# Half of a load moved forward on GpSimd's queue, and small corrections moved from VectorE to ScalarE, in a Fourier-mixing and channel-mix kernel

## The chip, the cores and the metric

The kernel runs on one core of a Trainium2 chip. The metric is the device time of one execution in microseconds (us). Every time was taken on one core, and every run was of the state called fast (no run was over 1.5% above the fastest of its kernel).

## The reference

Each of 8 batches (3072 rows of 256 columns) is Fourier-transformed along both axes, of which the real part is kept; a channel mix with the row before follows.

```python
X = np.fft.fft(x, axis=1)
x = np.fft.fft(X, axis=2).real
x_prev = np.concatenate([zeros, x[:, :-1, :]], axis=1)
xk = mu_k * x + (1.0 - mu_k) * x_prev
xr = mu_r * x + (1.0 - mu_r) * x_prev
k = np.maximum(xk @ w_k, 0.0)           # 256 -> 1024
v = k * k @ w_v                         # 1024 -> 256
r = 1.0 / (1.0 + np.exp(-(xr @ w_r)))   # 256 -> 256
return (r * v).astype(np.float32)
```

## The kernel before

The transform is done in stages on TensorE: A (sums over one index, by `a_sum` or, after a butterfly on VectorE, by `a_item`), D (`w_eo`, the transform along the columns) and C (tables `m1`, `m2`). VectorE forms the mixes, then K (`wk`), R (`wr`) and V (`wv`) are the products of the channel mix. All tables are computed on the chip during the first 43 us or so: angles on VectorE, sines on ScalarE, the last slices and the tables of the 128-row product (`tw`, `u128`) on GpSimd. GpSimd also issues every load of x and the weights, in the order of its program. K's weights come in two sets, and the rows of wk and wr are gathered in the order in which the transform leaves its columns.

```python
def loads():                                   # GpSimd's queue, at the start
    for a in range(2):
        next(row_part)                         # row numbers, 4 small operations
        gather(wk_sb[0][a], moe_w_k, a)
    nc.gpsimd.dma_start(out=wv_sb, in_=...)
    load_xh(1, 0)                              # batch 1's x, first half
    for a in range(2):
        gather(wr_sb[0][a], moe_w_r, a)
    load_xh(1, 1)
    next(row_part)
...
at(4, m_last)          # GpSimd: the last tables, four operations
at(4, loads_2)         # GpSimd: two gathers of wk, two of wr
at(5, plain_128)       # GpSimd: tw, u128
at(6, butterfly, 1, 1, 0)                      # VectorE
at(8, load_xh, 2, 0)   # GpSimd: batch 2's x
at(10, load_xh, 2, 1)
```

`eo_rest` writes two columns of `w_eo`; `m_ends` turns the sign of 64x64 pieces of `m1` and `m2` and zeroes a column of each. Both are on VectorE and are shown in the diff.

## Time and profile before

| | the kernel before |
|---|---|
| median of the first three timed runs (range) | 457.66 us (457.11 to 458.13) |
| the profiled execution | 455.39 us, span 453.6 us, clock 1.0 |
| TensorE busy | 444.9 us, 98% of the span |

The prediction below shows the lines of the shares, of the chain of waits up to stage D and of GpSimd's timeline at the start. GpSimd's timeline of the kernel before around 40 us (start, us, engine, line, operation, tiles, number, and in brackets the idle time before it with what ended it): the last gather of wr, three of the first four operations on `tw`, and batch 2's x.

```profile
35.48 0.95 POOL L364 DMA_INDIRECT wr<-in_moe_w_r_dram,row_i  x1 [0.30 <-issue]
...
38.60 1.25 POOL L407 TENSOR_SCALAR tw<-m 64x26 f16<-64x26 f16 x3 [0.20 <-issue]
...
43.48 1.15 POOL L104 DMA_DIRECT2D xh<-in_x_dram  x2
```

GpSimd has no idle time over 0.3 us here, and TensorE is busy without a gap from 44 to 80 us.

### The profile page before, as it was taken

What the parts mean: (1) busy time and instruction counts of PE and PEld (TensorE: products, weight loads), DVE (VectorE), ACT (ScalarE), POOL (GpSimd) and SP (SyncE); (2) the same over time, 40 slices, a digit from 0 to 9 for tenths busy, and PEclk for the clock granted to TensorE, in tenths of its full rate; (3) what the DMA queues carried; (4) which work ended last, traced back from release to release, by engine and by line L of the source; (5) the groups of instructions that cost most, each with busy time, mean ns of one, the idle gap of its engine ahead of it and who ended that gap; (6) DMA issues with size and microseconds to landing.
All of it is one profiled execution on the core that took longest, in us unless ns stands there. A gap on an engine that the chain in (4) does not pass through costs nothing.

```text
span 453.6 us, 9753 instructions
## 1 busy us (share of the span) xinstructions
PE 444.9 (98%) x4082; PEld 326.8 (72%) x4082; DVE 357.0 (79%) x499; ACT 360.7 (80%) x409; POOL 37.7 (8%) x71
## 2 busy tenths in 40 slices
PE   8899999999999999999999999999999999999995
PEld 5677777777777777777777777777777777676764
DVE  8999879977797869877788867887779755997453
ACT  7898997888778887888887888788878888666661
POOL 8748000000000000000000000000000000000000
PEclk9999999999999999999999999999999999999999
DMA  8975853537322572226522266122222222222223
GB/s 139 135 134 95 187 129 59 129 58 154 100 64 60 93 163 60 62 57 136 120 67 52 71 123 134 48 72 48 71 48 71 52 65 52 68 69 71 71 69 94
DMA packets 32412, 40.25 MB, mean 89 GB/s; under 512 B 3822, under 2 KB 29936, under 8 KB 31024
## 3 DMA queue, kind: packets, MB, share of 16 engines
q1 hardware_dynamic: 27776, 25.07, 22.0%
q0 software_dynamic: 4432, 14.42, 18.8%
q8 instruction: 32, 0.52, 0.5%
q10 hardware_dynamic: 160, 0.13, 0.1%
q14 instruction: 12, 0.10, 0.1%
HBM read 28.84 MB, written 25.17 MB: 119 GB/s over the span
## 4 chain that ended last, share of the span: by engine, by line
PE 94%; ACT 2%; DMA 1%; DVE 1%; issue 0%; POOL 0%; POOLq 0%
PE psV L623 37%; PE psW L585 36%; PE psW L609 9%; PE psW L458 4%; PE psW L434 4%; PE psW L489 3%; DMA xh<-in_x_dram 1%; ACT g_all L422 1%; ACT rl L595 1%; DVE a L420 1%; PE psW L448 1%; ACT L614 0%; ACT pq L422 0%; ACT r L614 0%; DVE rl L318 0%
## 5 line engine op out<-in xcount | busy, mean ns | idle before, releaser
L595 ACT ACTIVATE rl<-psW 128x1024 f16<-128x1024 f32 x192 | 196.4, 1026 | 79.6 <-PE psW L585 79.3
L623 PE MATMUL psV<-wv_sb,k 128*128 128x256 f16 x1536 | 198.6, 272 | 0.0
L585 PE MATMUL psW<-x,wk 128*128 128x512 f16 (+1 forms) x776 | 196.6, 377 | 0.3 <-ACT rl L595 0.3
L602 DVE TENSOR_TENSOR k<-rl 128x2048 f16<-128x2048 f16 (+1 forms) x98 | 117.5, 1202 | 61.3 <-ACT rl L595 60.6
L623 PEld LDWEIGHTS <-k 128*128 128x128 f16 x1536 | 143.7, 98 | 20.0
L585 PEld LDWEIGHTS <-wk 128*128 128x128 f16 x776 | 75.9, 98 | 50.2 <-issue 0.6
L633 DVE SCALAR_TENSOR_TENSOR o<-psV,r 128x512 f32<-128x512 f32 (+1 forms) x97 | 66.2, 683 | 23.8 <-PE psV L623 21.8
L554 DVE TENSOR_TENSOR x<-y,t 128x1536 f16<-128x1536 f16 x60 | 57.5, 958 | 2.1
L422 ACT ACTIVATE a<-psW 128x768 f16<-128x768 f32 x61 | 49.0, 806 | 1.6 <-PE psW L448 1.3
L609 PE MATMUL psW<-wr,x 128*128 128x256 f16 x384 | 49.8, 273 | 0.0
L614 ACT ACTIVATE r<-psW 128x1024 f16<-128x1024 f32 x48 | 49.0, 1020 | 0.8 <-PE psW L609 0.8
L609 PEld LDWEIGHTS <-x 128*128 128x128 f16 x384 | 37.6, 98 | 14.4
L422 ACT ACTIVATE g_all<-psW 128x1024 f16<-128x1024 f32 (+1 forms) x47 | 47.9, 1027 | 0.0
L117 DVE TENSOR_TENSOR eo<-xh 96x2048 f16<-96x2048 f16 x26 | 31.5, 1214 | 1.4 <-DMA xh<-in_x_dram 1.4
L458 PEld LDWEIGHTS <-a 128*128 128x128 f16 x384 | 25.0, 98 | 10.5 <-ACT a L422 0.6
L434 PEld LDWEIGHTS <-eo 96*128 96x128 f16 x416 | 23.4, 97 | 11.6
L104 POOL DMA_DIRECT2D xh<-in_x_dram x20 | 10.7, 539 | 222.6 <-DVE eo L117 221.7
L422 ACT ACTIVATE pq<-psW 128x896 f16<-128x896 f32 (+5 forms) x34 | 28.8, 851 | 0.5 <-PE psW L489 0.4
L458 PE MATMUL psW<-w_eo,a 128*128 128x128 f16 x376 | 28.3, 219 | 0.3 <-ACT rl L595 0.3
L434 PE MATMUL psW<-w_pm,eo 96*128 96x96 f16 x416 | 26.3, 205 | 0.0
L489 PEld LDWEIGHTS <-g_all 128*128 128x128 f16 x459 | 17.8, 98 | 8.4 <-ACT g_all L422 1.7
L489 PE MATMUL psW<-m,g_all 128*128 128x64 f16 x442 | 19.3, 193 | 0.9 <-ACT g_all L422 0.7
(107 smaller groups left out, 169.5 us busy)
## 6 DMA issues: line engine op xcount, KB each, us to landing
out_dram<-o SPq DMA_DIRECT2D x190, 128.0 KB, 2.4
xh<-in_x_dram POOLq DMA_DIRECT2D x14, 768.0 KB, 6.8
xh<-in_x_dram POOLq DMA_DIRECT2D x2, 384.0 KB, 5.3
xh<-in_x_dram POOLq DMA_DIRECT2D x4, 192.0 KB, 5.0
wv_sb<-in_moe_w_v_dram POOLq DMA_DIRECT2D x1, 512.0 KB, 8.6
out_dram<-o ACTq DMA_DIRECT2D x2, 64.0 KB, 2.0
out_dram<-o SPq DMA_DIRECT2D x2, 64.0 KB
y<-f SPq DMA_DIRECT2D x7, 3.4 KB
```

The lines of the kernel that those rows point to most:

```text
L422: nc.scalar.activation(out=out_ap, in_=in_ap, func=AF.Copy)
L434: nc.tensor.matmul(out=ps[:, 128 * i:128 * i + 96], lhsT=eo[:, 8 * j + i, e, :], rhs=w_pm[0:96, 0], start=True, stop=True)
L458: nc.tensor.matmul(out=_v(ps, 256 * i + 64 * (1 - e), [(128, 2), (1, 64)]), lhsT=a_t[b][:, e, 2 * u:2 * u + 2, :], rhs=w_eo[:, e, :], star ...
L489: nc.tensor.matmul(out=ps[:, o + 64 * i:o + 64 * i + 64], lhsT=g_all[:, u, col:col + 128], rhs=m[:, sl] if sl != 1 else mz[:, 0 if m is m1 ...
L554: V.tensor_tensor(out=dst, in0=_v(y_t[b], 64 * (NSL * a + lo + 3 * m), [(1, n)]), in1=_v(x_t["t", a], 64 * lo, [(1, n)]), op=ALU.subtract ...
L585: nc.tensor.matmul(out=st["k", ds][:, 512 * hs + lo:512 * hs + hi], lhsT=wk_sb[m][a][:, 128 * fc:128 * fc + 128], rhs=xk[:, a, 512 * i + l ...
L595: nc.scalar.activation(out=st["rl"][:, 2 * ds:2 * ds + 2], in_=st["k", ds].rearrange("p (f t) -> p f t", f=2), func=AF.Relu, bias=0.0, sca ...
L602: V.tensor_tensor(out=k2_t[c][:, lo:hi], in0=r, in1=r, op=ALU.mult)
L609: nc.tensor.matmul(out=ps[:, 256 * tb:256 * tb + 256], lhsT=x_t[b, 1, m][:, a, 512 * i + 128 * tb: 512 * i + 128 * tb + 128], rhs=wr_sb[m] ...
L614: nc.scalar.activation(out=st["r", c], in_=ps, func=AF.Sigmoid)
L623: nc.tensor.matmul(out=st["v", tb - h][:, 256 * h:256 * h + 256], lhsT=k2_t[c][:, fc, 128 * tb:128 * tb + 128], rhs=wv_sb[:, fc], start=(f ...
L633: V.scalar_tensor_tensor(out=o.rearrange("p a b -> p (a b)")[:, 0:256 * n], in0=st["v", t0][:, 0:256 * n], scalar=16.0, in1=st["r", c][:, ...
```

## The change

Its intent: VectorE ends stage A of batch 0 late, so the two corrections of w (`eo_rest`) and of the tables (`m_ends`) go to ScalarE, into its waits, and the last part of the second angles goes behind stage A. The first half of batch 1's first x is put at the head of the queue, right behind batch 0's x.

```diff
--- before.py
+++ after.py
@@ -333,14 +333,15 @@
         V.tensor_scalar(out=m2[lo64, s0:s1], in0=m1[hi64, s0:s1], scalar1=-1.0, scalar2=None,
                         op0=ALU.mult)
         V.tensor_copy(out=m2[hi64, s0:s1], in_=m1[lo64, s0:s1])
+        if s0 == 0:
+            for m in (m1, m2):
+                V.memset(m[:, 0, 0:1], 0.0)
 
     def m_ends():
 
 
-        for n, m in enumerate((m1, m2)):
-            V.tensor_scalar(out=m[hi64, 0], in0=m[hi64, 0], scalar1=-1.0, scalar2=None,
-                            op0=ALU.mult)
-            V.memset(m[:, 0, 0:1], 0.0)
+        for m in (m1, m2):
+            nc.scalar.activation(out=m[hi64, 0], in_=m[hi64, 0], func=AF.Copy, scale=-1.0)
 
     def m_zero():
         for n, m in enumerate((m1, m2)):
@@ -366,12 +367,15 @@
 
     V.memset(mz, 0.0)
 
+    xh_t[1, 0] = xh_pool.tile([96, 16, 256], FP16, name="xh")
+
     def loads():
+        load_part(1, 0, 0, 8)
         for a in range(2):
             next(row_part)
             gather(wk_sb[0][a], moe_w_k, a)
         nc.gpsimd.dma_start(out=wv_sb, in_=moe_w_v.rearrange("(fc p) v -> p fc v", p=128))
-        load_xh(1, 0)
+        load_part(1, 0, 8, 8)
         for a in range(2):
             gather(wr_sb[0][a], moe_w_r, a)
         load_xh(1, 1)
@@ -391,8 +395,8 @@
     def eo_rest():
 
         for col, sign in ((63, 0.5), (127, -0.5)):
-            V.tensor_scalar(out=w_eo[:, 0, col:col + 1], in0=w_eo[:, 0, 127:128], scalar1=sign,
-                            scalar2=0.5, op0=ALU.mult, op1=ALU.add)
+            nc.scalar.activation(out=w_eo[:, 0, col:col + 1], in_=w_eo[:, 0, 127:128],
+                                 func=AF.Copy, bias=0.5, scale=sign)
 
     def plain_128():
 
@@ -644,6 +648,7 @@
 
     loads()
     eo_sine()
+    eo_rest()
     a_sum(0, 0, 0)
     a_sum(0, 0, 4)
     keep_busy(1)
@@ -655,11 +660,10 @@
     a_sum(0, 1, 0, "V")
     a_sum(0, 1, 4)
     m_zero()
-    eo_rest()
-    m_angles(22, NSL)
     a_sum(0, 1, 8)
     a_sum(0, 1, 12, "V", 2)
     a_sum(0, 1, 14, "A", 2)
+    m_angles(22, NSL)
     m_ends()
     mu_turn()
     d_half(0, 0, ps_v(), "A")
```

## The prediction

> **What bounds the kernel now.** The kernel takes 457.66 us (457.11 to 458.13); the profiled execution has a span of 453.6 us, all at the full granted clock. I read the page's shares first.
>
> ```profile
> PE 444.9 (98%) x4082; PEld 326.8 (72%) x4082; DVE 357.0 (79%) x499; ACT 360.7 (80%) x409; POOL 37.7 (8%) x71
> PE 94%; ACT 2%; DMA 1%; DVE 1%; issue 0%; POOL 0%; POOLq 0%
> ```
>
> The second line is the chain that ended last. TensorE is busy for 98% of the span and is 94% of that chain. The rest of the chain (ACT, DVE, DMA) lies almost all before 40 us, and every line of the diff works there, before 20 us or so. So the change cannot touch the steady part: it can only shift its start. All of TensorE's idle time is 453.6 - 444.9 = 8.7 us; by stretches, 1.55 us of it is before 6 us, 0.52 in 6 to 12 us and 1.33 in 12 to 20 us. A gain can come above all out of these last two.
>
> Next I read the chain of waits in order of time up to 40 us (columns: start, us, what).
>
> ```profile
> 8.18 0.85 PE psW L448 x8
> 9.05 0.96 DVE a L420
> 10.01 0.40 DVE rl L318
> 10.44 0.44 DVE m L333
> 10.91 0.73 DVE m L335
> 11.68 0.96 DVE a L420
> 12.64 0.07 DVE w_eo L394
> 12.73 0.16 DVE w_eo L394
> 12.89 0.40 DVE rl L318
> 13.29 0.48 DVE a L420
> 13.90 0.61 PE psV L458 x8
> ```
>
> From 9.05 to 13.77 us VectorE is the bound: its last piece of stage A (L420, ended 13.77) waits behind the two corrections of w (L394) and a part of the second angles (L318), and stage D (L458) starts at 13.90 only because of it. This is what the change goes for. Last I read the timeline of GpSimd, which issues all loads, with the first use of wk on TensorE beside it (columns: start, us, engine, line, what).
>
> ```profile
> 6.64 1.39 POOL L192 TENSOR_SCALAR unit<-pcol_i 2x1 f32<-2x1 int32 x2
> 8.12 0.71 POOL L290 TENSOR_SCALAR row<-pcol_f 128x1 f32<-128x1 f32 x1
> 10.11 1.28 POOL L364 DMA_INDIRECT wk<-in_moe_w_k_dram,row_i  x1 [0.29 <-POOL row_i L293]
> 12.95 1.29 POOL L364 DMA_INDIRECT wk<-in_moe_w_k_dram,row_i  x1 [0.27 <-POOL row_i L298]
> 14.23 0.99 POOL L373 DMA_DIRECT2D wv_sb<-in_moe_w_v_dram  x1
> 15.20 0.61 POOL L104 DMA_DIRECT2D xh<-in_x_dram  x1
> 19.19 3.62 PEld L585 LDWEIGHTS <-wk 128*128 128x128 f16 x26
> ```
>
> To see here: GpSimd is a strict queue that runs without a pause from 1.26 to 20.9 us; behind the row numbers (L290 to L298) it issues wk's two gathers, wv, then batch 1's x. TensorE takes up wk at 19.19 us without waiting for it.
>
> [...] So a load with an unmet wait holds up everything behind it on GpSimd. The trace before has no such case among these loads (no idle of GpSimd there over 0.3 us); it has the mild form, the wk gather waiting 0.29 us for its row numbers. [...] L290 took 0.71 us beside VectorE's wrap of the angles (8.01 to 8.74), the like operations after it 0.27, 0.24 and 0.21. [...] The trace before shows gaps of at most 0.63 us after the start and no fall; the gap that I predict is near 1.2 us, so I count nothing for it.
>
> **The change part by part.**
> (1) w's corrections to ScalarE, right behind its sine (5.22 to 5.73). ScalarE then waits 1.28 us for TensorE until 7.01; two operations of one column at 0.20 us each (its 128x1 activation at 2.04 took that) fit in. Cost 0; VectorE's chain loses 12.64 to 12.89, 0.25 us.
> (2) The last angles (0.40 us in the chain) go behind VectorE's last piece of A: that piece ends 0.65 us sooner in all, less some 0.08 for the two memsets (0.06 each, overlapping) that now come before the A evictions: about 13.77 - 0.57 = 13.2.
> (3) m's sign corrections go to ScalarE behind its last A eviction, which ends at 13.30. Two 64x64 operations at 0.20 us (mz's two took 0.39) end at 13.70, before stage D's first result could be there. Hidden.
> Stage D then waits for ScalarE's eviction at 13.30 and for TensorE's small mu products, whose modelled end is 13.35: it starts at about 13.42 in place of 13.90. **Gain: about 0.5 us**, which the chain D, C, K would carry on to K's first product, 18.7 in place of 19.2.
> (4) The load of batch 1's first half is put ahead of the row numbers on GpSimd. The buffer is that of batch 0's first x (two buffers, two halves in use), and the built program has the load wait for TensorE's count 43, ten warm-up products plus all 33 up to the end of L448's fourth group, the buffer's last reader. In the trace that count arrives at 9.69 us. GpSimd is free at 8.05. So it stands still for 1.65 us, issues for 0.55 (its loads of x take 0.53 to 0.66) and starts L290 at 10.3 in place of 8.12: **2.2 us later**, and L290 then meets VectorE's angles, swap and copy (9.93 to 11.64), so 2.0 to 2.7 after the blocking is counted. All gathers shift with it. The first wk gather goes from 10.11 to about 12.35, the second from 12.95 to about 15.25.
>
> When does wk land? In the trace's landing records the first gather's last increment is at 14.81, 4.70 us after its start; of the second's, at least 17.59, 4.64 after (11 of its 16 are missing). The second would land at 15.25 + 4.64 = 19.9 (19.5 to 20.4). K's second product needs it; before, that ran at about 19.3 with 1.7 us of slack. The shift of 2.2 to 2.3 us eats this slack and 0.6 us more. So K starts at about 19.9, TensorE standing idle from 18.8, and **the 0.5 us of (1) to (3) ends in this wait**.
> After that, ScalarE is busy for 8.00 of the 8.00 us from 20 to 28 and TensorE for 7.82 of the next 8.00, so a late K isn't caught up. wv (landed 22.88, used at 25.00) moves by 2.3 but has less x beside it and is used 0.6 later: about even. The gain of the early half of x is nil: L448 took it up at 27.68 without a wait, as all of it had landed at 26.70.
> Sum: -0.5 (hidden) and +0.6 at K: 457.66 + 0.6 = **458.3 us**.
>
> **The rivals.**
> Rival A, the intent: wk lands in time and the 0.5 us stays. For it: part of the second gather's 4.64 us may be queueing, the DMA engines stand nearly idle at 11 and at 14 us, and few landings are recorded; the row operations may slip through between VectorE's. It needs the shift plus the flight to be 1.2 us shorter than I have it. It makes 457.66 - 0.5 = 457.2.
> Rival B, the wait is longer: GpSimd's row operations are blocked up to 11.64 by VectorE's swap, and the x load of 384 KB (some 2 us at the 200 GB/s that x's loads show) is ahead of wk's packets. Then wk lands at 20.5 and wv too comes late (25.5 against 25.2). For it: the 1.2 us that GpSimd's second operation of L192 took against 0.22 of the first; against it: the engines should be through with that half by 13.1 us, before wk's first packet. It makes +1.2 to +1.5, 459.0.
> Rival C, no engine or wait matters: the gain and the wait cancel and the result is 457.7.
>
> **Range and chances.** The three medians lie within 1.1 us of each other: 457.2 (a quarter), 457.7 to 458.5 (half), 459 (a quarter), each with run-to-run noise of some 0.5 us, as the times before spread. So 458.3 with a range from 456.9 to 459.3. 2% is 9.2 us, more than all of TensorE's idle time, so a gain of that size is out of the question; a loss of it would need a wait ten times my estimate or a fallen clock. Chances: faster 0.01, within 2% 0.98, slower 0.01.
>
> **What would show it.** Right: L394's successors stand on ScalarE before 7 us; stage D starts near 13.4; GpSimd's new load starts near 9.7 behind a wait for TensorE of about 1.6 us; the second wk gather starts near 15.2; the first L585 weights (a shifted line number) show a wait for a DMA of about 1 us and start near 19.9; a total within 1 us of before. Wrong: no idle time of TensorE ahead of K (then rival A, and the step that failed is the landing of wk); GpSimd not held at the new load (then the wait on count 43 was misread); stage D still at 13.9 (then the gain of (1) to (3) was not there to lose); or a wait at wv's first use (rival B).

Where a cut is marked, the text held a statement on the hardware that no trace or run shows. The sum came to -0.5 (hidden) and +0.6 at K, 457.66 + 0.6 = 458.3 us. Three of its arguments need their numbers beside them. That a load with an unmet wait holds up what stands behind it on GpSimd was taken for granted; the changed kernel's trace shows it: GpSimd stands 1.99 us for TensorE ahead of the new load, and L290 behind it starts at 10.64 us in place of 8.12. What is called blocking there is read from the durations alone: L290's 0.71 us, and L402, an operation of one column too, took 1.26 us beside VectorE's square (36.60 to 37.81 us) in the kernel before and 0.25 us in the profile of only_moves (L403 there, at 38.62 us), where it came after the square; in the changed kernel L290 and L291 took 0.38 and 0.39 us beside the swap and the copy. And that a gap near 1.2 us costs no clock was my assumption; the trace has no such gap after the start. In the rivals, the DMA engines that "stand nearly idle" have a share of 0.31 from 11 to 12 us and of 0.27 from 14 to 15, and x's loads moved 184 to 205 GB/s from 4 to 10 us.

## The result

The changed kernel takes **455.44 us** (455.23 to 456.17, six executions), against 457.38 us (456.85 to 458.13, six) of the kernel before in the same rounds. The ratio is 0.996 with a 95% interval of 0.9947 to 0.9974. Here and below, a ratio is the mean time of one kernel's runs over that of the other's of the same rounds, so not quite the ratio of the medians that I quote. The class, within 2%, is as predicted; the time is 1.5 us below the low end of the range.

The profiled execution of the changed kernel took 456.13 us (span 454.4), that is 0.74 us **more** than the profiled one of the kernel before. Its shares and the engines of its chain:

```profile
PE 444.6 (98%) x4082; PEld 326.6 (72%) x4082; DVE 356.1 (78%) x495; ACT 361.7 (80%) x413; POOL 38.1 (8%) x72
PE 92%; DMA 2%; ACT 2%; POOL 1%; issue 1%; DVE 0%; POOLq 0%
```

TensorE is as busy as before, and DMA and POOL have come into the chain. Where, the chain of waits of the changed kernel shows (start, us, what):

```profile
10.02 0.56 POOL xh L104
...
12.43 1.10 POOL wk L365
...
15.05 4.97 DMA wk<-in_moe_w_k_dram,row_i
20.07 1.39 PE psW L589 x11
```

The early half of x is followed by the gathers of wk, and the second gather's landing (15.05 + 4.97 = 20.02) releases K. The timelines of the same kernel, of GpSimd, ScalarE and TensorE in this order:

```profile
10.02 0.56 POOL L104 DMA_DIRECT2D xh<-in_x_dram  x1 [1.99 <-PE psW L452]
15.05 1.07 POOL L365 DMA_INDIRECT wk<-in_moe_w_k_dram,row_i  x1 [0.27 <-POOL row_i L298]
```
```profile
5.76 0.44 ACT L398 ACTIVATE w_eo<-w_eo 128x1 f16<-128x1 f16 x2
13.39 0.40 ACT L344 ACTIVATE m<-m 64x64 f16<-64x64 f16 x2
```
```profile
13.42 0.62 PE L462 MATMUL psV<-w_eo,a 128*128 128x128 f16 x8
20.07 4.42 PE L589 MATMUL psW<-x,wk 128*128 128x256 f16 x27 [0.54 <-DMA wk<-in_moe_w_k_dram,row_i]
```

Stage D starts at 13.42 us in place of 13.90, but GpSimd stood 1.99 us for TensorE ahead of the new load, and K now waits 0.54 us for wk. Every step in the trace is the one predicted, and yet the timed runs are 2 us faster. So the gain is in executions that these two traces don't show, and the experiments had to find those.

### The profile page after: what moved, and what is told of

The parts are those of the page before. It is cut to its first block, busy times and chain, and to the rows that moved or that the text cites. A ratio compares the mean times of both kernels' runs of the same rounds, so it can differ in the third digit from the quotient of the medians.

```text
span 454.4 us, 9755 instructions
## 1 busy us (share of the span) xinstructions
PE 444.6 (98%) x4082; PEld 326.6 (72%) x4082; DVE 356.1 (78%) x495; ACT 361.7 (80%) x413; POOL 38.1 (8%) x72
## 4 chain that ended last, share of the span: by engine, by line
PE 92%; DMA 2%; ACT 2%; POOL 1%; issue 1%; DVE 0%; POOLq 0%
PE psV L627 37%; PE psW L589 35%; PE psW L613 9%; PE psW L462 4%; PE psW L438 4%; PE psW L493 3%; ACT rl L599 1%; DMA xh<-in_x_dram 1%; DMA wk<-in_moe_w_k_dram,row_i 1%; PE psW L452 1%; ACT g_all L426 0%; ACT L618 0%; POOL xh L104 0%; POOL wk L365 0%; ACT r L618 0%
```

## The experiments

Seventeen runs were made, five of them repeats of a kernel; the runs of one call share a chip and the runs of the kernel before, and each call had another chip. Where its row in a table says "before", those are the shared runs. Each timed run of five rounds gives six executions (a_third seven), the first of which is the profiled one.

### First call: both kernels again, and the two halves of the change

`b_again` and `a_again` are the kernels before and after, unchanged. 

> The kernel before once more, unchanged, for the spread of its own executions and a second trace: the first profiled execution took 455.39 us, 2.0 us less than the median of the timed ones (457.38). Theory 1 (margin of the loads): most executions hold a wait of about 2 us that the first trace lacks, for a load of batch 1's x or of a weight; then a slow trace shows TensorE idle before 40 us behind a load and the times scatter over 455.4 to 458. Theory 2 (clock): the slow executions have the same waits, but products at half rate for longer at the start. Theory 3 (profile): profiling itself shortens the execution; then this trace is again near 455.4 beside timed runs of 457.4, with the same waits.

The half rate at the start is in the trace of the kernel before: the ten warm-up products begin 0.42 us apart, and two of the same size at 17.06 us 0.21 us apart (the granted clock reads 1.00 in both stretches).

> The changed kernel once more. All theories: 455.2 to 456.2 as before, with about 0.8 us of waiting for the second wk gather ahead of the first K product in the trace. Theory 1: no other new wait at a load. If theory 3 held, the profiled execution would be some 2 us shorter than the timed ones, which the changed kernel's first look did not show (456.13 against 455.44).

`only_load` is the kernel before with the load part alone, `only_moves` the changed kernel with the loads of before.

```diff
     def loads():
+        load_part(1, 0, 0, 8)
         ...
-        load_xh(1, 0)
+        load_part(1, 0, 8, 8)
```

Of the change's diff, only_load has these lines (and the tile that they need) and no other; only_moves has all others and not these.

> Only the load part of the change: the first half of batch 1's x ahead of the row numbers, all corrections and angles as before. Theory 1: this half brings the gain, 455.5 us or so against 457.4 before, by taking away the wait for batch 1's x. If the moves of corrections and angles bring the gain instead: 457.4 plus up to 1.2 us, since the second wk gather comes 2.1 us later and nothing is gained.

> Only the corrections on ScalarE and the later angles; loads as before. Theory 1: stage D starts 0.5 us sooner, near 13.4 us, and K near 18.7, but batch 1's x comes no sooner, so the whole is 456.9 to 457.4 against 457.4. If the moves bring the gain: 455.4 us.

| | median us | over 456.5 us | profiled us |
|---|---|---|---|
| before | 455.48 | 5 of 11 | |
| b_again | 459.45 | 5 of 6 | 459.74 |
| a_again | 455.78 | 2 of 6 | 455.15 |
| only_load | 455.42 | 1 of 6 | 455.81 |
| only_moves | 457.25 | 4 of 6 | 457.04 |

One and the same kernel, before, runs at 455.2 and at 461.6 us. The ratios say little (b_again against before: 1.0035, interval 0.9978 to 1.0093), but the profiles of `b_again` and `only_moves` fell on long executions. That alone ends theory 3 of b_again: a profiled execution can be long. What theory 1 looked for is there, but at 56 us and not before 40; of theory 2, the slow clock is there (granted at 0.50 from 60 to 62 us), behind the gap and not at the start. Busy time by stretch, first of the kernel before in its short execution, then of b_again (the columns are the stretch; its length; busy us with counts of PE, PEld, DVE, ACT and POOL; granted TensorE clock; DMA share; GB/s):

```profile
54.00:60.00 6.00, 6.00 (x71) 4.71 (x68) 4.76 (x6) 6.00 (x8) 0.51 (x1) 1.00 0.75 153
60.00:66.00 6.00, 6.00 (x78) 4.58 (x76) 3.84 (x8) 5.91 (x9) 0.00 (x0) 1.00 0.53 139
```
```profile
54.00:60.00 6.00, 3.24 (x32) 2.36 (x30) 5.40 (x6) 3.35 (x5) 0.00 (x0) 0.97 0.68 153
60.00:66.00 6.00, 6.00 (x57) 4.16 (x55) 5.43 (x8) 4.28 (x6) 0.51 (x1) 0.74 0.94 167
```

In the long execution TensorE stands for 6.00 - 3.24 = 2.76 us in the first stretch, and in the second its clock is granted at 0.74, which is worth 6.00 x 0.26 = 1.56 us (0.18 more at 0.97 in the first). The sum is 4.50 us. Ahead of the gap b_again was 0.25 us early (its first product of V starts at 24.75 us, that of before at 25.00), and 4.50 - 0.25 = 4.25 is the difference of the spans, 457.8 - 453.6. In only_moves the same stretch has a busy time of 4.24 us, so a gap of 1.76, but the clock stays at 1.00 in both stretches, and its time is 2.0 us above its two short executions (454.98 and 455.02). So long executions seem to come in two heights, with and without a fallen clock. Of the 37 long executions of the kernel before, the 14 from 458.78 us up all have a mean clock of 0.991 to 0.996; of the 17 below that have a clock on record, one has (457.85 us, 0.993).

What makes the gap is in the chain of waits of b_again:

```profile
36.47 6.08 DMA wr<-in_moe_w_r_dram,row_i
...
42.69 0.67 POOL tw L407
...
47.90 6.65 DMA xh<-in_x_dram
...
54.57 1.22 DVE eo L117
...
57.49 0.97 DVE x L554
...
58.51 0.94 PE psW L609 x7
```

Read it downwards. The last gather of wr starts at 36.47 us and lands at 42.55. GpSimd's second operation on `tw` waits for that landing. The code has no use of wr there, so why it waits is not explained; but in none of the profiles does that operation start ahead of the landing (38.60 behind 38.47 us in the short execution). Batch 2's x stands behind it in the queue, so it is issued at 47.90 and lands at 54.55. VectorE's butterfly waits for it, and behind the butterfly in VectorE's queue stand the mixes that TensorE's product R needs. In the short execution of the kernel before, TensorE holds this stretch of the chain alone. GpSimd's timeline of b_again answers to the three lines of before:

```profile
36.47 2.03 POOL L364 DMA_INDIRECT wr<-in_moe_w_r_dram,row_i  x1 [0.30 <-issue]
...
42.69 1.92 POOL L407 TENSOR_SCALAR tw<-m 64x26 f16<-64x26 f16 x3 [2.98 <-DMA wr<-in_moe_w_r_dram,row_i]
...
47.90 1.14 POOL L104 DMA_DIRECT2D xh<-in_x_dram  x2
```

The gather starts 1.0 us later than in the short execution and takes 2.03 us in place of 0.95. Of the 1.0 us, 0.5 come from the last tables ahead of it on GpSimd (3.09 us in place of 2.58) and 0.4 from the second gather of wk (1.40 in place of 0.99). It starts with VectorE's square (at 36.47 us, 1.22 us long); in the short one it started 1.12 us ahead of the square (35.48 against 36.60). The square took no longer for it (1.22 us against 1.21). A gather of wr took 2.02 or 2.03 us when it started together with the square (the last gather in four profiles), some 1.95 when it started just behind the start of a butterfly (33.23 us in the kernel before, the butterfly at 33.14; 33.99 and 33.90 in the changed kernel), and 0.94 or 0.95 when it started within the output step (35.48 us, the step from 35.41 to 36.69). Why, the traces don't show. Ending 2.2 us later against the first output store, the gather also meets the stores of 128 KB: the first was issued at 35.98, the gather's issue ended at 38.50, and its landing at 42.55 falls beside that of the fourth store, 42.78. In the short execution its issue ended 0.32 us behind the first store's, and it landed 2.0 us after that. Why it lands so much later is not shown.

All 19 profiles (those of both kernels, and one of each of the 17 runs) fall into two classes by this measure. In 15 the gather's issue ends at most 0.32 us behind the first store's, and it lands 1.7 to 2.3 us after its end. In four it ends 2.52 or 2.53 us behind it and lands 3.4 to 4.1 us after its end: b_again, only_moves, after_gather_late and plain_late. I call this **losing the race**.

My working theory R from here on: long executions are those that lose this race; the change does not touch what the gap costs but makes the loss rarer. Rivals: the gap has another cause and the race goes with it by chance, or the difference between the two kernels is luck.

### Second call: take the wait away, lose the race by force, and copy K's delay

`plain_late` is the kernel before with the GpSimd work on `tw` queued behind batch 2's x, so that the load no longer stands behind the wait; the race itself is left alone. `moves_plain_late` is the same on only_moves.

```diff
-    at(5, plain_128)
+    at(10, plain_128)          # behind load_xh(2, 1)
```

> The kernel before, with one thing moved: GpSimd's preparation for the later batches (w plain again, the twiddles) stands behind the loads of batch 2's x in its queue, in place of ahead of them. Theory R (race on GpSimd): the slow executions of the kernel before come from the last gather of wr[...] when it comes 0.7 us later against VectorE; its late landing holds the twiddles, these hold batch 2's x (issued at 46.9 to 47.9 in place of 43.5), VectorE stands before it and TensorE idles 1.8 to 2.8 us near 56. Here the loads don't stand behind that landing any more: x of batch 2 is issued before 41 us, no execution is slow, all lie within 455.1 to 455.8. Theory X (batch 1's x is what comes late): nothing here changes when that comes, so slow executions stay, as many as of the kernel before (16 of 23 over 456.5).

> The same, with the corrections on ScalarE and the later angles besides, but without the early half of x. Theory R: no slow execution, and the 0.3 to 0.5 us that the moves gain show in all: 454.8 to 455.2, less than both kernels. Theory X: slow executions stay.

`after_gather_late` is the changed kernel with three memsets of a scratch tile on GpSimd ahead of the second gathers, which delays them so that the race must be lost.

```diff
+        for _ in range(3):
+            nc.gpsimd.memset(idle, 0.0)    # at the end of m_last
```

> The changed kernel, with three idle memsets on GpSimd (about 0.3 us each) ahead of the second set of gathers, so that these come 1 us later against VectorE. Theory R: slow as often as the kernel before, most executions over 456.5, and a trace with the last wr gather taking some 2.0 us to issue in place of 0.95, batch 2's x issued after 46.5, a gap of TensorE of 1 to 3 us near 56. Theory X: 1 us on GpSimd here matters to nothing, 455.1 to 456.2 as the changed kernel.

`before_k_late` is the kernel before with four idle matmuls ahead of K, which copies the wait for wk without moving a load.

```diff
+            keep_busy(4)
             k_products(chunks[0], 0, 0, 256)
```

> The kernel before, with four idle products (0.215 us each) ahead of K's first, so that K and VectorE's chain behind it come 0.7 to 0.9 us later while GpSimd's chain, which hangs on the landing of wr near 27.2, does not. Theory R: the race is won more often, so that less than a third of the executions are slow, and the fast ones take 0.8 more than the fast ones of before: 456.0 to 456.3. Theory X: all executions 0.8 us longer and as many slow ones: a median near 458.

| | median us | over 456.5 us | profiled us |
|---|---|---|---|
| before | 456.42 | 5 of 11 | |
| plain_late | 455.17 | 1 of 6 | 455.12 |
| moves_plain_late | 455.30 | 0 of 6 | 455.17 |
| after_gather_late | 460.09 | 6 of 6 | 459.89 |
| before_k_late | 455.91 | 2 of 6 | 455.75 |

Forcing the loss makes every execution of the changed kernel long, 458.23 to 461.32 us (ratio 1.0064, interval 1.0012 to 1.0115). GpSimd's timeline of that kernel has the picture of b_again:

```profile
36.66 2.02 POOL L368 DMA_INDIRECT wr<-in_moe_w_r_dram,row_i  x1 [0.30 <-issue]
...
48.10 1.14 POOL L104 DMA_DIRECT2D xh<-in_x_dram  x2
```

And the profile of plain_late happened to lose the race, but lost nothing by it, because x is already out of the queue:

```profile
36.46 2.03 POOL L364 DMA_INDIRECT wr<-in_moe_w_r_dram,row_i  x1 [0.30 <-issue]
38.48 1.14 POOL L104 DMA_DIRECT2D xh<-in_x_dram  x2
```

It took 455.12 us. So the way from a late gather to a long execution is shown, from both sides. `before_k_late` has 2 of 6 long, fewer than before's 5 of 11, which is no proof with such counts. Its profile shows that a delay of K can go with a won race.

plain_late and moves_plain_late differ by the moves alone, and the gain of the moves does not show in them: 455.17 and 455.30 us, with V's first product at 24.74 and 24.81 us in their profiles. The 454.8 to 455.2 expected of the second was missed.

### Third call: which part of the load helps

`load_behind_wk` is the changed kernel with the early half of x moved behind the gathers of wk, so that K is on time again.

```diff
     def loads():
-        load_part(1, 0, 0, 8)
         for a in range(2):
             next(row_part)
             gather(wk_sb[0][a], moe_w_k, a)
+        load_part(1, 0, 0, 8)
```

> The whole change, but the first half of batch 1's x stands on GpSimd's queue behind both gathers of wk instead of ahead of them: it is still ahead of the gathers of wr and of what batch 2 needs, but no longer makes K wait. Theory R, in its form that the early load helps because K's wait for wk lets GpSimd's chain (the last tables, the wr gathers) win the race against VectorE's square: K is on time again (second product near 19.0 us, no wait for wk), so long executions come back, some 2 to 4 of 6 over 456.5 us, and the short ones are 0.5 us below those of the change, about 454.6 to 455.0 us. Rival R2, the early load helps because GpSimd has one load less to issue between and after the gathers and so starts its later chain sooner: none or one of 6 over 456.5 us, base 454.6 to 455.0 us. Rival R3, K's wait costs nothing to the end: the short ones stay at 455.2 to 455.6 us.

`moves_plain_again` repeats the kernel of moves_plain_late and `a_third` the changed kernel.

> The candidate that beat both: the change without its early load, and with the 128-row plain product's GpSimd work queued later, behind batch 2's x. The same kernel as moves_plain_late. Theory R: batch 2's x is issued ahead of the wait for the last wr gather, so losing the race costs nothing: none of 6 over 456.5 us, all within 454.7 to 455.6 us, median 0.3 us below the change run beside it. Rival, its six short executions were luck: two or more of 6 over 456.5 us.

> The change unchanged, for more executions beside the two others. Theory R: none to two of 6 over 456.5 us, median near 455.5 us, the profiled execution with K's second product at about 20.0 us. If its gain over the kernel before were luck, as often long as the kernel before (21 of 34 executions so far): about four of 6 over 456.5 us.

| | median us | over 456.5 us | profiled us |
|---|---|---|---|
| before | 455.32 | 3 of 11 | |
| load_behind_wk | 455.50 | 1 of 6 | 454.56 |
| moves_plain_again | 455.35 | 1 of 6 | 455.32 |
| a_third | 455.48 | 1 of 7 | 458.45 |

With K on time load_behind_wk had one long execution, where 2 to 4 were expected if K's wait were needed for the rare losses. That speaks against this form of theory R, as far as six executions can. Two of its executions, 454.56 and 454.60 us, are faster than any of the change; in its profile D starts at 13.14 us and V at 24.19, so here the gain of the moves arrives. The others, at 455.4 to 456.0, I can't explain.

In this call the kernel before had few long executions, and then the change is no faster (455.48 against 455.32). And the profile of a_third is long without any gap near 56 us. It is a second kind, seen in TensorE's timeline at the start:

```profile
9.50 2.76 PE L452 MATMUL psW<-w_pm,xh 96*128 96x192 f16 x26 [1.75 <-DMA xh<-in_x_dram]
```

Batch 0's first x came late. TensorE stood 1.75 us for it (0.54 in the first profile of the change), and its clock was at 0.79 from 8 to 16 us, worth 8 x 0.21 = 1.7 us. Together that is 1.2 + 1.7 = 2.9 us of the 3.0 by which this execution is above the median of the change's short ones, 455.46. The early half of x can't have caused it, as it was issued later, at 11.29 us, and the race was won here.

### Fourth and fifth call: the landing of wr alone, and a last candidate

The last tables of GpSimd start 0.35 us after the first gathers of wr have landed in the profile of before (27.21, then 27.56). If the early half helps because wr lands earlier, moving wr forward should do the same. `wr_first` puts it ahead of x and wv, `moves_wr_first` and `moves_wr_plain` do so with the moves and with the later `plain_128` besides.

```diff
-        nc.gpsimd.dma_start(out=wv_sb, in_=...)
-        load_xh(1, 0)
         for a in range(2):
             gather(wr_sb[0][a], moe_w_r, a)
+        load_xh(1, 0)
+        nc.gpsimd.dma_start(out=wv_sb, in_=...)
```

> The kernel before with one reordering on GpSimd's queue: the two gathers of wr stand ahead of batch 1's x and of wv in place of behind them, so that they should land near 22 us in place of 27.2 us; nothing else differs, K is on time and wk is not touched. Theory R2 (the last tables start 0.35 us after the landing of wr, and whether they come in time decides the race for the last gather of wr): the tables start as soon as VectorE's swap is done, near 26.3 us, the chain ends about 1.2 us earlier, the last gather always wins: none or one of 6 over 456.5 us, the others at 455.0 to 455.5 us as in the short executions of the kernel before, and no gap of TensorE near 56 us in the profiled one. Rival, long executions have another cause than this race (such as a late first x) and the landing of wr has no part in them: 2 to 4 of 6 over 456.5 us, as in the kernel before. Risk: wv lands near 27.3 us, and the first product that needs it stands at 28.5 us; if it is late the base rises.

> The same reordering with the moves to ScalarE and of the second angles, without the early half of x: a candidate that beats both kernels. Theory R2: the moves' 0.5 us shows, since K doesn't wait for wk, and the race is won: none or one of 6 over 456.5 us, the others at 454.6 to 455.0 us, 0.5 us below the short executions of the change. Rival (other cause of the long ones): 2 to 4 of 6 over 456.5 us.

> As the last, with the 128-row plain product's GpSimd work behind batch 2's x besides. Theory R2: the race is already won, so the second remedy adds nothing: 454.6 to 455.0 us, none or one of 6 over 456.5 us. If it has clearly fewer long executions than the run without it, the race was still being lost there.

| | median us | over 456.5 us | profiled us |
|---|---|---|---|
| before | 457.62 | 6 of 11 | |
| wr_first | 457.27 | 4 of 6 | 455.96 |
| moves_wr_first | 456.30 | 3 of 6 | 456.53 |
| moves_wr_plain | 456.27 | 1 of 6 | 456.17 |

The risk that was named came in: TensorE waited for wv, as its timeline in wr_first shows.

```profile
25.83 1.03 PE L623 MATMUL psV<-wv_sb,k 128*128 128x256 f16 x8 [0.78 <-DMA wv_sb<-in_moe_w_v_dram]
```

I had also misread the first product that needs wv: it stands at 25.00 us in the kernel before, not at 28.5. In the profiles of moves_wr_first and moves_wr_plain that wait was 1.79 and 1.69 us. It lifts the short executions, and puts the one of moves_wr_first at 456.53, in which the race was won, over the line. But even so wr_first had four long executions, so the early landing of wr did not do away with them. The profile shows why it does little: the last tables start at 26.21 us, 1.35 us earlier than before, and then take 3.15 us in place of 2.58 beside VectorE's work; the last gather starts at 34.93, only 0.55 us earlier.

`wr_mid` moves the gathers of wr ahead of batch 1's x only, behind wv; `behind_plain` is load_behind_wk with the later `plain_128`; `a_fourth` is the changed kernel.

```diff
-        load_xh(1, 0)
         for a in range(2):
             gather(wr_sb[0][a], moe_w_r, a)
+        load_xh(1, 0)                  # wr_mid
```

> The kernel before with the two gathers of wr one place forward only, behind wv and ahead of batch 1's x, so that wv lands in time (the run with wr ahead of both stalled TensorE 0.78 us on wv and still had 4 of 6 long). wr should land near 23.5 us, x near 27 us, just ahead of the first product that needs it, at 27.7 us. Theory R2 (the landing of wr alone decides): none or one of 6 over 456.5 us, the others at 455.0 to 455.5 us. Rival R4 (starting the tables earlier only puts them beside VectorE's two-input work, so that they lose there what they gained; what counts is where the last gather of wr meets VectorE): 2 to 4 of 6 over 456.5 us, and a last gather of about 2 us again in the profiled execution.

> The candidate put together from what the runs showed: the change with its early half of x behind the gathers of wk (K on time, two executions of 454.6 us) and with the 128-row plain product's GpSimd work behind batch 2's x (no wait for the last wr ahead of that load). If both act as read: 454.5 to 455.0 us with none or one of 6 over 456.5 us, some 0.7 us below the change beside it. If the executions of 455.4 to 456.0 us of the run without the second edit come from elsewhere, they stay, and the median is 455.3 to 455.6 us.

> The change unchanged, beside the candidate and for the count: so far 3 of its 19 executions are over 456.5 us, against 30 of 56 of the kernel before. Expected none to two of 6, the others at 455.0 to 456.2 us. If its advantage were luck of the first chips: three or more of 6.

| | median us | over 456.5 us | profiled us |
|---|---|---|---|
| before | 456.72 | 7 of 11 | |
| wr_mid | 455.71 | 2 of 6 | 456.52 |
| behind_plain | 455.47 | 2 of 6 | 454.75 |
| a_fourth | 455.97 | 1 of 6 | 456.03 |

wr_mid's two long executions are 456.52 and 456.72, and five of before's seven are above 457; its ratio is 0.9969 (0.994 to 0.9998). The one of 456.52 is the profiled one, and it is a third kind: it won the race and has no gap near 56 us, but its clock was at 0.57 from 14 to 18 us, worth 4 x 0.43 = 1.7 us (mean clock of the execution 0.996), and K's first product came at 20.28 us. This leans towards the landing of wr having a part, against wr_first, and I leave it open. behind_plain has the lowest time of all, 454.46, and two long executions of 457.85 and 459.05 us without a profile (mean clock 0.994 and 0.992).

**No version clearly beats the change.** moves_plain_late is the nearest: twelve executions have a median of 455.34 and one long, beside 455.54 and 4 of 25 for the change; run side by side the medians were 455.35 and 455.48.

## Why the prediction was wrong

Executions of the same kernel by call, number over 456.5 us:

| call | kernel before (with b_again) | changed kernel |
|---|---|---|
| first result | 6 of 6 | 0 of 6 |
| first | 10 of 17 | 2 of 6 |
| second | 5 of 11 | |
| third | 3 of 11 | 1 of 7 |
| fourth | 6 of 11 | |
| fifth | 7 of 11 | 1 of 6 |
| all | 37 of 67 | 4 of 25 |
| median of the short ones | 455.32 us | 455.46 us |

The first result overstates the change, and that is luck: with 37 of 67 over all, six long ones of six are more than this kernel's usual share. In the later calls the medians of change and before were 455.78 and 455.48, 455.48 and 455.32, 455.97 and 456.72 us, and none of the three ratios is clear of 1 (intervals 0.9931 to 1.0027, 0.996 to 1.0013, 0.9947 to 1.0004). Without the first result, from which the theory came, the counts are 31 of 61 and 4 of 19.

- **"Gain: about 0.5 us"** of the moves was right in its mechanism and in the first pair of traces, and about twice too large over all. In the pair, stage D starts at 13.42 us, the number predicted, in place of 13.90; w's corrections stand on ScalarE at 5.76, the tables' at 13.39. But D starts at 13.40 to 14.00 us (median 13.58) in the seven profiles without the moves, and at 13.06 to 13.53 (median 13.33) in the eleven with them, a_third with its late first x left out. The 13.90 was one of the latest; the gain at D is 0.25 us, and plain_late and moves_plain_late don't show it at the end.
- **"K starts at about 19.9"** was right for the first trace: 20.07 in the profiled execution, with the second gather at 15.05 (predicted 15.25) and its landing at 20.02. GpSimd's idle time for TensorE was 1.99 us against 1.65 predicted. In other executions of the change the wait differs: none in a_again, 0.95 us in a_fourth.
- **"the 0.5 us of (1) to (3) ends in this wait"** fits, but no run shows it apart. The short executions of the two kernels differ by 455.46 - 455.32 = 0.14 us. That is rival C for the short ones ("no engine or wait matters"); the +0.6 of the sum was 0.74 in the two profiled executions and 0.14 over all.
- **The step that failed is the sum, "457.66 + 0.6".** The +0.6 came from a trace of 455.39 us, a short execution, and was added to a median of executions that were all long. What makes 457.66 out of 455.39 was not in the trace, and I took it for noise "of some 0.5 us". The later runs put a gap of TensorE near 56 us in its place, of 1.76 to 2.76 us in the three profiles that hold it, with or without a fall of the clock.
- **"So the change cannot touch the steady part: it can only shift its start"** and **"The gain of the early half of x is nil"** failed with it. The order on GpSimd reaches 56 us, through the last gather of wr, `tw` and batch 2's x. Of the 37 and 4 long executions the gain consists: 0.14 us worse when short, but seldom long.
- None of the rivals had this in it. B, a longer wait, was 3.6 us from the result on the wrong side; A came to 457.2 for another reason. ("The three medians lie within 1.1 us" is a slip: 457.2 to 459.0 is 1.8.)
- The clock: I counted nothing for a gap near 1.2 us, and none of that length came: in the first profile of the change the longest gap from 6 us on is 0.87 us (at 17.1 us), the one ahead of K is 0.54, and the clock was granted at 1.00 in every stretch up to 80 us, as in that of the kernel before. The length of one gap did not decide whether the clock fell. It fell after 2.76 us (b_again), after 1.75 us behind a first stretch that had gaps too (a_third, granted 0.55 from 11 to 13 us), and in wr_mid with no gap over 0.97 us from 5 us on (0.57 from 14 to 18 us). Of the three gaps near 56 us, two cost clock and the one of 1.76 us (only_moves) did not. Each of these falls is worth about 1.7 us, by the same arithmetic as above.

**Shown:** the long executions that were profiled with the gap near 56 us lose the race; forcing the loss makes all six long; taking the load out from behind the wait leaves a lost race harmless (one profile). **Inferred:** that most of the 37 long executions of the kernel before lost the race, as one of them has a profile (b_again), and late first loads or a clock that falls at the start, as in a_third and wr_mid, can be among them; that the first six executions of the kernel before were of this kind, as none of them has a profile; their times, 456.85 to 458.13, are the lower of the two heights. In the four profiles of the changed kernel the race is won each time, in the two of the kernel before once. **Open:** by which way the early half makes the loss rarer. only_load has 1 of 6 and only_moves 4 of 6, so it is the load part that carries it, as far as six executions tell. K's wait alone (before_k_late, 2 of 6) and the early landing alone (wr_first 4 of 6, wr_mid 2 of 6) each do less or are unclear, and the early load without K's wait (load_behind_wk) has 1 of 6. Open too are the 5 long ones among 30 executions of the versions in which the load doesn't stand behind the wait; none of them was profiled. All five have a mean clock of 0.991 to 0.996, so a fall of the clock is in them, as in a_third and wr_mid.

## What to carry to other kernels

Compare the profiled execution's own time with the timed ones before any trace is read: where they differ by more than the effect that is looked for, the trace lacks what the median holds. Look for a load that stands in a queue behind a wait for another load, as a microsecond lost by the first can become several at the second (here the gather of wr started 1.0 us later and batch 2's x was issued 4.4 us later, 47.90 in place of 43.48); putting the load ahead of the work that waits made a lost race harmless here (plain_late), which does not depend on winning it. With executions of two kinds, count the kinds as well as comparing medians, since a median jumps between them.
